# A windowed-attention block on one core: five equal score sets of 64-key pieces, E by V in 64x32 tiles over two banks, masks as a minimum on VectorE

## The chip, the cores and the metric

The kernel runs on one core of one Trainium2 chip. The metric is the device time in microseconds, a median over several runs. One execution was also recorded by the hardware profiler; all rows of the profile come from that one.

The engines are named as in the profile: PE (matrix products; PEld is its loading of the stationary operand, which is counted apart and overlaps), DVE (vector), ACT (activation functions and copies), POOL (general), SP (here it only issues DMAs). Matrix products write to PSUM, from which DVE and ACT read; all else lies in SBUF, 128 partitions wide. ACT and POOL can issue DMAs too; the profile then calls them ACTq and POOLq, as it calls SP's SPq.

## The reference

The block computes attention and an MLP, both behind a layer norm whose scale, shift and gate come from a vector c:

```python
mod = (_silu(c) @ w_mod).reshape(c.shape[0], 6, 1, -1)     # sa, ca, ga, sb, cb, gb
h = _layernorm(x) * (1 + ca) + sa
x = x + ga * _A_ref(h, wqkv, wo)                            # attention
h = _layernorm(x) * (1 + cb) + sb
x = x + gb * _B_ref(h, w_gate, w_up, w_down)                # (sigmoid(h @ w_gate) * (h @ w_up)) @ w_down

# in _A_ref: S = 2048, D = 640, H = 32, Dh = 20, W = 256
q, k, v = (h @ wqkv) split into 3 x H heads of Dh
scores = einsum('bhqd,bhkd->bhqk', q, k) * Dh ** (-0.5)
mask = (idx[:, None] - idx[None, :] >= 0) & (idx[:, None] - idx[None, :] < W)
p = softmax(where(mask, scores, -1e9))
o = einsum('bhqk,bhkd->bhqd', p, v) -> (S, D) @ wo
```

Each query sees itself and the 255 keys before it. x is 2048 x 640, the MLP's inner width is 1536, all inputs are bf16.

## The kernel before

The 2048 tokens are cut in eight chunks a = 0 to 7 of 256. A chunk goes through: layer norm statistics and normalisation (`ln_stats`, L785 ff., the normalised x is written at L815), turning to hT with tokens in columns and applying scale and shift (`modulate`, `pe_transposes`), projections to q, k and v with evictions from PSUM (`evac`, L914 on ACT, L915 on DVE), attention, the output projection, the second norm, the MLP (gate and up products in `h2T` by `wg` and `wu`, then `hh` by `wd`), and the gated sums. Weights are loaded once. The modulation vectors are computed at the start and while chunk 0 runs; gates are folded into the weights wo and wd (L1333, L1270).

Attention of a chunk is done in two halves q of sixteen heads. Head 16q + 4j + k lies with its 20 rows of Q and K at partitions 32j, so four heads go through four row groups of PE together. The scores are computed with keys on partitions and queries on columns, so that exp's output E is at once the moving operand of E by V. A half's scores go set by set into one PSUM tile S of four banks (pool `p_S` holds one such tile, 2048 columns), and each set is emptied by one exp on ACT over 128 x 2048 (L1067, L1041, in chunk 0 L1104). No maximum is subtracted; a column of ones beside V gives the sum of a row.

For chunks 1 to 7 `main_set` computes for four heads everything but the two ends of the window, in 24 matmuls with 64 keys each, two column groups at a time; `ends_set` computes for all sixteen heads of the half the first and the last 64 columns, in 32 matmuls with 128 keys. Four main sets and one ends set make a half. The masks are POOL's affine_select: each main set has two that write 128 x 256 pieces to a buffer G (L1072) and two on 128 x 512 in place (L1076), each ends set two on 128 x 1024 (L1045). Chunk 0 has no keys before it, and six sets in all (`score_set`, masks at L1112).

`burst` multiplies E by V for a half: 64 matmuls (32 in chunk 0) with 128 keys on the rows and 32 columns of V as weights, in four column groups, into two PSUM banks X. With `AFTER = 1` the burst of a half stands right before the second score set of the next half (`with_pv`), in chunk 0 (`NOW = 1`) by itself. `norm` transposes the result and divides (L1162 to L1166).

On every engine the order is fixed. The program is recorded as operations with the engines they may go to; `PLAN`, a list of numbers (operation times five plus engine), sets on which engine each runs and in which order; buffers of a pool are handed out in that same order, and semaphore waits are worked out from the dependencies. So attention's matmuls stand among those of the MLP and of the projections of neighbouring chunks, which fill PE while ACT works on a set. A list `FETCH` of 40 times stands for other DMA traffic in the planner's model of the DMA queues. POOL's operations also wait for the last DVE operation marked `port` before them. All of PE's products are issued by two helpers, `mm` at L698 (128 x 128 tiles) and L699 (smaller tiles). All DMAs are issued at L584 and, transposing, at L822.

These lines give the pieces of a main set and E by V in the old form:

```python
    PIECES = (((0, 0, 0, 256, 0), (-1, 64, 0, 256, 256)), ((-1, 0, 0, 192, 256), (0, 64, 64, 192, 64)),
              ((1, 0, 128, 64, 448), (-2, 64, 64, 64, 0)))
...
                for kb, q0, n, side, c0 in ((0, 0, 256, 0, 0), (-2, 0, 128, 1, 0), (1, 128, 128, 1, 128), (-1, 0, 256, 0, 256)):
...
                        ins = mm(e, X[bank].ap[32 * j:32 * j + 32, oc:oc + n], V[2 * a + kb].ap[:, h * VW:h * VW + 32],
                                 src, (bank, j) not in seen, True, tp=(0, 32 * j))
```

## Time and profile before

| | us |
|---|---|
| median of three runs | 324.63 |
| the runs | 323.03 to 324.86 |
| span of the profiled execution | 321.8 |
| PE busy | 315.6 |
| ACT busy | 213.9 |
| DVE busy | 198.8 |
| POOL busy | 189.5 |
| 16 DMA engines, mean rate | 102 GB/s |

The span goes from the first to the last instruction of the profiled execution; the page gives no other time of that execution. Busy times are sums over an engine's instructions. In rows of groups, the parts are: line, engine, operation, output and inputs by their names, shapes, count, then busy time, the mean length of one in ns, and the idle time of the engine just before them with what ended it. A row of the timeline has the start, the length, the line and the count of instructions put together; the length of the last matmul of such a row reaches into the next row, since matmuls overlap, so a stretch is best measured from start to start.

### The profile page before, as it was taken

What the parts mean: (1) busy time and instruction counts of PE and PEld (TensorE: products, weight loads), DVE (VectorE), ACT (ScalarE), POOL (GpSimd) and SP (SyncE); (2) the same over time, 40 slices, a digit from 0 to 9 for tenths busy, and PEclk for the clock granted to TensorE, in tenths of its full rate; (3) what the DMA queues carried; (4) which work ended last, traced back from release to release, by engine and by line L of the source; (5) the groups of instructions that cost most, each with busy time, mean ns of one, the idle gap of its engine ahead of it and who ended that gap; (6) DMA issues with size and microseconds to landing.
All of it is one profiled execution on the core that took longest, in us unless ns stands there. A gap on an engine that the chain in (4) does not pass through costs nothing.

```text
span 321.8 us, 11465 instructions
## 1 busy us (share of the span) xinstructions
PE 315.6 (98%) x5045; PEld 236.8 (74%) x5045; DVE 198.8 (62%) x424; ACT 213.9 (66%) x229; POOL 189.5 (59%) x349
## 2 busy tenths in 40 slices
PE   6999999999999999999999999999999999999996
PEld 2677767677877777766777677877877777877885
DVE  4689987877886746584555555465534474386323
ACT  2699997877787986768686867676976746411220
POOL 3338759878768493949484848577575826601000
PEclk9999999999999999999999999999999999999999
DMA  7999999999922534126526100220800004002101
GB/s 249 348 262 278 223 179 248 194 225 295 206 36 43 88 75 55 44 63 108 77 19 111 37 22 2 63 42 25 132 18 4 22 22 104 20 5 61 43 0 41
DMA packets 62123, 32.92 MB, mean 102 GB/s; under 512 B 45946, under 2 KB 60794, under 8 KB 62074
## 3 DMA queue, kind: packets, MB, share of 16 engines
q1 hardware_dynamic: 59904, 29.73, 43.5%
q10 hardware_dynamic: 2170, 2.46, 2.8%
q8 instruction: 39, 0.64, 0.9%
q14 instruction: 10, 0.08, 0.1%
HBM read 18.68 MB, written 2.62 MB: 66 GB/s over the span
## 4 chain that ended last, share of the span: by engine, by line
PE 96%; DMA 1%; DVE 1%; ACT 1%; issue 0%; ACTq 0%
PE M L698 79%; PE S L699 8%; PE M L699 7%; DMA x<-in_A_x_dram 1%; ACT hT L831 1%; DVE st L793 1%; PE S L698 1%; PE S L690 0%; ACT stg L914 0%; ACTq L584 0%; DVE x L815 0%; DVE st L795 0%; ACT hT L914 0%; DVE x L1308 0%; DVE mA L778 0%
## 5 line engine op out<-in xcount | busy, mean ns | idle before, releaser
L1067 ACT ACTIVATE E<-S 128x2048 bf16<-128x2048 f32 x56 | 105.0, 1875 | 40.6 <-PE S L699 40.2
L1072 POOL TENSOR_SCALAR_AFFINE_SELECT E<-E 128x256 bf16<-128x256 bf16 x112 | 46.6, 427 | 57.1 <-ACT E L1067 25.1
L1076 POOL TENSOR_SCALAR_AFFINE_SELECT E<-E 128x512 bf16<-128x512 bf16 x112 | 70.6, 646 | 4.6 <-DVE x L815 1.2
L698 PE MATMUL M<-h2T,wg 128*128 128x256 bf16 x480 | 67.0, 273 | 0.0
L698 PE MATMUL M<-h2T,wu 128*128 128x256 bf16 x480 | 66.7, 273 | 0.0
L1289 DVE SCALAR_TENSOR_TENSOR hh<-sig,M 128x512 bf16<-128x512 f32 x48 | 32.4, 678 | 42.9 <-ACT sig L1287 26.4
L698 PE MATMUL M<-wd,hh 128*128 128x320 bf16 (+2 forms) x396 | 57.1, 295 | 0.0
L698 PEld LDWEIGHTS M<-h2T,wg 128*128 128x128 bf16 x480 | 45.4, 98 | 7.8 <-DVE T L1162 0.2
L698 PEld LDWEIGHTS M<-h2T,wu 128*128 128x128 bf16 x480 | 45.2, 98 | 7.3
L1287 ACT ACTIVATE sig<-M 128x512 f32<-128x512 f32 x48 | 28.5, 595 | 31.2 <-PE M L698 30.9
L698 PEld LDWEIGHTS M<-wd,hh 128*128 128x128 bf16 x396 | 37.2, 98 | 13.7 <-DVE hh L1289 0.2
L1045 POOL TENSOR_SCALAR_AFFINE_SELECT E<-E 128x1024 bf16<-128x1024 bf16 x28 | 32.0, 1147 | 4.9 <-ACT E L1041 3.4
L699 PEld LDWEIGHTS S<-QT,KT 20*64 20x64 bf16 (+1 forms) x1856 | 20.0, 100 | 17.4 <-issue 9.7
L699 PE MATMUL S<-QT,KT 20*64 20x256 bf16 (+5 forms) x1856 | 32.3, 228 | 0.4 <-issue 0.4
L1041 ACT ACTIVATE E<-S 128x2048 bf16<-128x2048 f32 x14 | 26.3, 1876 | 6.8 <-PE S L699 6.7
L793 DVE BATCH_NORM_STATS2 st<-x 128x6 f32<-128x320 bf16 x64 | 28.9, 479 | 2.4 <-DMA x<-in_A_x_dram 1.8
L1162 DVE STREAM_TRANSPOSE T<-M 128x512 f32<-128x512 f32 x32 | 21.5, 700 | 12.9 <-PE S L699 11.6
L698 PE MATMUL M<-wk,hT 128*128 128x320 bf16 x160 | 27.9, 299 | 0.0
L1308 DVE TENSOR_TENSOR x<-M,x 128x320 bf16<-128x320 f32 (+2 forms) x33 | 15.4, 475 | 18.8 <-PE M L698 18.6
L698 PE MATMUL M<-wq,hT 128*128 128x320 bf16 x160 | 26.2, 299 | 0.7 <-DVE hT L832 0.5
L698 PE MATMUL M<-wv,hT 128*128 128x320 bf16 x160 | 26.0, 299 | 0.0
L698 PE MATMUL M<-wo,oT 128*128 128x320 bf16 x160 | 25.9, 299 | 0.0
(84 smaller groups left out, 356.4 us busy)
## 6 DMA issues: line engine op xcount, KB each, us to landing
x<-in_A_x_dram SPq DMA_DIRECT2D x18, 160.0 KB, 3.7
wd<-in_w_mod_dram SPq DMA_DIRECT2D x6, 320.0 KB, 5.4
wd<-in_B_w_down_dram SPq DMA_DIRECT2D x4, 480.0 KB, 5.5
wu<-in_w_mod_dram SPq DMA_DIRECT2D x5, 320.0 KB, 4.8
x<-in_A_x_dram ACTq DMA_DIRECT2D x8, 160.0 KB, 2.7
out_dram<-x SPq DMA_DIRECT2D x8, 160.0 KB, 1.9
wu<-in_B_w_up_dram SPq DMA_DIRECT2D x2, 576.0 KB, 4.7
wg<-in_B_w_gate_dram SPq DMA_DIRECT2D x2, 576.0 KB, 6.8
```

Of the source, the lines that this page charges most:

```text
L698: return e.matmul(o, l, r, start=st, stop=sp, skip_group_check=True)
L699: return e.matmul(o, l, r, start=st, stop=sp, tile_position=tp, skip_group_check=True)
L793: A("dve", lambda e, g, bi=bi, j=j: e.bn_stats(v(bi * 12 + j * 6, 6), src[bi].ap[:, j * 320:(j + 1) * 320]), 0.48, reads=[src[bi].r()], wr ...
L1041: A("act", lambda e, eng: e.activation(cell().rearrange("p m (x c) -> p m x c", c=64)[:, :, 0:4:3, :], Sp.ap[:].rearrange("p j (k x c) -> ...
L1045: A("pool", lambda e, eng, c0=c0, pat=pat, base=base, cm=cm: e.affine_select(cell()[:, :, c0:c0 + 64], cell()[:, :, c0:c0 + 64], pattern=p ...
L1067: A("act", lambda e, eng: e.activation(part(0, 512), Sp.ap[:], ACT.Exp, scale=SM_SCALE), 1.876, reads=[Sp.r()], writes=[E.r("C"), E.r("B") ...
L1072: A("pool", lambda e, eng, hc=hc, src=src, far_h=far_h: e.affine_select(side(hc), part(src, 64), pattern=[[0, 4], [-1 if far_h else 1, 64] ...
L1076: A("pool", lambda e, eng, c0=c0, near=near: e.affine_select(part(c0, 128), part(c0, 128), pattern=[[0, 4], [1 if near else -1, 128]], com ...
L1162: A("dve", lambda e, g, h=h: e.transpose(T1.ap[:, 512 * h:512 * h + 512], X[h].ap), 0.694, reads=[X[h].r()], writes=[T1.r(h)], prio=3.5, t ...
L1287: A("act", lambda e, g, pg=pg, sg=sg: e.activation(sg.ap[:], pg.ap[:], ACT.Tanh, scale=0.5), c_act(512), reads=[pg.r()], writes=[sg.r()], ...
L1289: A("dve", lambda e, g, pu=pu, sg=sg, f0=f0: e.scalar_tensor_tensor(out=hh.ap[:, f0:f0 + 2, :], in0=sg.ap[:].rearrange("p (a b) -> p a b", ...
L1308: A("dve", lambda e, g, ps=ps, bi=bi, c0=c0, n=n: e.tensor_tensor(x1[bi].ap[:, c0:c0 + n], ps.ap[:, 0:n], x1[bi].ap[:, c0:c0 + n], op=ALU. ...
```

## The change

For chunks 1 to 7 a half now has five equal score sets (`SETS`) in place of four and one. A piece is 64 keys by at most 256 queries, and each half of PE's columns (64 wide) takes its own heads. The first two sets have two pieces of 256 columns in each tile, the next two have pieces of 192, 64, 64 and 192, the fifth four of 128 (`ONE`, `TWO`, the last line of `SETS`). Chunk 0 has two sets of 192, 64 and 256 a half and one that both halves share. `run` issues the matmuls of the eight tiles in turn, by columns done. Over the whole program score matmuls go from 1856 to 1920.

E by V now uses tiles of 64 rows and 32 columns: each of the eight tiles (two row halves, four column groups) goes through the eight pieces of its head, the upper half of the rows into one PSUM bank of X and the lower into the other. A burst has 128 matmuls in place of 64 (64 in place of 32 in chunk 0), 1920 over the program in place of 960.

For this a head's V rows of one 64-key piece must lie in the right half of the partitions: the V projection reads wv's columns with a stride, and each V tile is evicted in twice as many pieces of 64 partitions (64 in place of 32).

The masks are a minimum of E with a table `mk`, on DVE: 79 tensor_tensor operations in place of POOL's selects. The table holds 0 or 3e38, and is made at the start by 9 instructions on POOL and DVE. G goes; there are 8 buffers for E in place of 6.

In `ln_stats` the normalisation of x may go to DVE or POOL for every chunk but the pieces done one by one at the start; with the new plan 12 of 32 are on DVE (26 before) and 20 on POOL (6 before).

```diff
-NE = 6
+NE = 8
 EW = 2048
+BIG = 3.0e38
...
+            if not one:
+                A("pool", lambda e, g: e.tensor_tensor(v(32, n), st.ap[:, 24:28].rearrange("p (b t) -> p b t", t=2)[:, :, 0], v(30, n),
+                                                       op=ALU.mult), 0.26,
...
+            A("dve" if one else ("dve", "pool"), xh, {"dve": 0.44, "pool": 0.87}, port=True,
...
-                    ps.ap[:, 0:320], hT[a].ap[:, kt, bi * 128:(bi + 1) * 128], wv[:, kt, half * 320:half * 320 + 320]))
+                    ps.ap[:, 0:320].rearrange("p (g c) -> p g c", c=40), hT[a].ap[:, kt, bi * 128:(bi + 1) * 128],
+                    wv[:, kt, :].rearrange("p (g c) -> p g c", c=80)[:, :, 40 * half:40 * half + 40])) for kt in range(NDT)]
...
+                for odd in range(2):
+                    evac(lambda b=b, half=half, odd=odd: heads(V[b].ap[64 * half:64 * half + 64, 352 * odd:352 * odd + 352], VW)[:, :, 0:DH],
+                         lambda ps=ps, odd=odd: heads(ps.ap[64 * odd:64 * odd + 64, 0:320], DH), 320, [ps.r()], [V[b].r((half, odd))], 6.5,
...
+    def run(e, prog, emit):
+        at = {t: p[0] for t, p in prog.items()}
+        pos = dict.fromkeys(prog, 1)
+        ins = None
+        while pos:
+            t = min(pos, key=lambda t: (at[t], list(prog).index(t)))
+            what = prog[t][pos[t]]
+            if isinstance(what, int):
+                at[t] = max(at[t], what)
+            else:
+                ins = emit(e, t, what)
+                at[t] += what[-1]
+            pos[t] += 1
+            if pos[t] == len(prog[t]):
+                del pos[t]
+        return ins
+
+    ONE = ((-1, 0), (0, 256))
+    TWO = ((-2, 0), (-4, 192), (3, 256), (1, 320))
+    SETS = (([(h, x, c) for x, c in st] for st in (ONE, TWO) for h in range(2)))
+    SETS = [list(x) for x in SETS] + [[(h, x, c + 256 * h) for h in range(2) for x, c in ((-3, 0), (2, 128))]]
+    MASKS = [(192, 512, 4, 128, 64)] * 2 + [(128, 512, 4, 256, 0)] * 2 + [(64, 256, 8, 128, 64)]
+    FIRST = ((1, 0), (3, 192), (0, 256))
+
+    def piece(x):
+        q0 = 64 * max(0, x)
+        return x // 2, x % 2, q0, 64 * min(4, x + 5) - q0
...
+            prog = {(j, half): [0] + [(q, h, x, c, piece(x)[3]) for q, h, x, c in parts] for j in range(4) for half in range(2)}
...
+                return mm(e, Sp.ap[64 * half:64 * half + 64, j, c:c + n], keys_of(a, kb, 64 * odd, gi, j, 64),
+                          QT[a].ap[32 * j:32 * j + DH, gi, q0:q0 + n], True, True, tp=(32 * j, 64 * half))
...
+                return e.tensor_tensor(v, v, mk[:, m0:m0 + w].unsqueeze(1).to_broadcast([128, g, w]), op=ALU.min)
+            A("dve", fn, c_dve(g * w, 2.0), port=True, reads=[E.r(), R_mk], writes=[E.r()], prio=5, tag=f"mask{a}")
...
+        mine = [(h, x) + where[a, q, h, x] for h in range(2) for x in ((-1, 0, -2, 1, -3, 2, -4, 3) if a else (0, 1, 2, 3))]
...
+                ins = mm(e, X[half].ap[32 * j:32 * j + 32, h * 256 + q0:h * 256 + q0 + n],
+                         V[2 * a + kb].ap[64 * half:64 * half + 64, v0:v0 + 32],
+                         E.ap[64 * half:64 * half + 64, j * 512 + c:j * 512 + c + n], t not in seen, True, tp=(64 * half, 32 * j))
```

`PLAN` is new as a whole. Its numbers count other operations than before, so its lines say nothing; the order that comes out of it does. In the changed kernel L706 and L707 are the two matmul helpers, L581 the DMAs, L1071 the masks, L920 the evictions on DVE, L1110 and L1112 `norm`'s first steps.

On PE, around a burst E by V of an early chunk, before (weights' and moving columns behind the names):

```order
L698 MATMUL M<-h2T,wg 128x256 x10
L699 MATMUL M<-E,V 32x256 x4
L699 MATMUL M<-E,V 32x128 x8
L699 MATMUL M<-E,V 32x256 x8
L699 MATMUL M<-E,V 32x128 x8
L699 MATMUL M<-E,V 32x256 x8
L699 MATMUL M<-E,V 32x128 x8
L699 MATMUL M<-E,V 32x256 x8
L699 MATMUL M<-E,V 32x128 x8
L699 MATMUL M<-E,V 32x256 x4
L699 MATMUL S<-QT,KT 64x256 x8
L699 MATMUL S<-QT,KT 64x192 x8
```

and of the changed kernel, with the score set that follows the burst:

```order
L707 MATMUL M<-E,V 32x256 x16
L707 MATMUL M<-E,V 32x192 x16
L707 MATMUL M<-E,V 32x128 x16
L707 MATMUL M<-E,V 32x64 x16
L707 MATMUL M<-E,V 32x256 x16
L707 MATMUL M<-E,V 32x192 x16
L707 MATMUL M<-E,V 32x128 x16
L707 MATMUL M<-E,V 32x64 x16
L707 MATMUL S<-QT,KT 64x256 x16
L706 MATMUL M<-wd,hh 128x320 x8
L706 MATMUL M<-wo,oT 128x320 x5
```

The burst stands at the same place, ahead of a score set, with twice the matmuls, in pieces of 256, 192, 128 and 64 columns; the set behind it has 16 matmuls there in place of 24.

The masks on POOL before, with a step of the norm (L800, L802) between them:

```order
L1072 AFFINE_SELECT E<-E 128x4x64 x2
L800 TENSOR_SCALAR st<-st 128x2
L1076 AFFINE_SELECT E<-E 128x4x128 x2
L802 TENSOR_TENSOR st<-st,mhalf 128x2
L1072 AFFINE_SELECT E<-E 128x4x64 x3
L1045 AFFINE_SELECT E<-E 128x16x64
```

and on DVE in the changed kernel, about chunk 0's end:

```order
L1071 TENSOR_TENSOR E<-E,mk 128x4x256 x2
L803 BN_AGGR st<-st 128x2
L1186 TENSOR_TENSOR x<-M,x 128x320
L1071 TENSOR_TENSOR E<-E,mk 128x4x128
L920 CAST V<-M 64x16x20
L1186 TENSOR_TENSOR x<-M,x 128x320
L1071 TENSOR_TENSOR E<-E,mk 128x8x128
```

The masks have moved from a queue with little beside them to the one that also evicts V and adds the residual (L1186).

On SP the first DMAs, before:

```order
L584 DMA wq<-in_A_wqkv_dram 128x3x320
L584 DMA x<-in_A_x_dram 128x640
L584 DMA wd<-in_w_mod_dram 128x1280 x5
L584 DMA wq<-in_A_wqkv_dram 128x5x320
L584 DMA wq<-in_A_wqkv_dram 128x2x320
```

and in the changed kernel (wd is here a buffer that w_mod goes through):

```order
L581 DMA wk<-in_A_wqkv_dram 128x5x320
L581 DMA x<-in_A_x_dram 128x640
L581 DMA wd<-in_w_mod_dram 128x1280 x5
L581 DMA wq<-in_A_wqkv_dram 128x3x320
L581 DMA x<-in_A_x_dram 128x640
```

A half of wk has come to the front, and the first part of wq stands behind w_mod.

248 lines of the change are left out of this document (77 added, 171 removed), and 217 rows, old and new, of the table PLAN.

## Prediction

> **What bounds the kernel now.** I read the page first: the busy line, the slices of PE and the shares of the chain.
>
> ```profile
> span 321.8 us, 11465 instructions
> PE 315.6 (98%) x5045; PEld 236.8 (74%) x5045; DVE 198.8 (62%) x424; ACT 213.9 (66%) x229; POOL 189.5 (59%) x349
> ...
> PE   6999999999999999999999999999999999999996
> ...
> PE 96%; DMA 1%; DVE 1%; ACT 1%; issue 0%; ACTq 0%
> ```
>
> Then the table of busy time by stretch (columns: PE, PEld, DVE, ACT, POOL with instruction counts, then the granted clock, the DMA share and GB/s).
>
> ```profile
> 0.00:14.00 14.00, 10.54 (x94) 5.42 (x95) 6.62 (x23) 5.61 (x12) 5.28 (x24) 1.00 0.91 292
> 14.00:50.00 36.00, 35.60 (x603) 25.26 (x603) 32.01 (x76) 33.34 (x43) 22.71 (x40) 1.00 1.06 243
> 50.00:100.00 50.00, 50.00 (x866) 36.89 (x864) 39.43 (x92) 39.07 (x41) 38.53 (x70) 1.00 0.91 188
> 300.00:321.80 21.80, 19.41 (x178) 16.55 (x176) 6.45 (x12) 3.59 (x6) 0.00 (x0) 1.00 0.08 24
> ```
>
> PE idles 3.5 us in the first 14, 2.4 in the tail, 0.4 between 14 and 50 and not at all from 50 to 300, at full clock. The time is therefore startup, plus the PE work, plus the tail. What PE no longer has to do is gained; work on another engine is free until PE waits for it. The span of 321.8 lies 2.8 below the median of 324.63, and I carry this 2.8 over.
>
> **E by V.** The PE timeline around one burst (start, length, instructions):
>
> ```profile
> 105.49 1.50 PE L699 MATMUL M<-E,V 128*32 128x256 bf16 x64
> 106.93 0.43 PE L699 MATMUL S<-QT,KT 20*64 20x256 bf16 x24
> 107.29 0.61 PE L698 MATMUL M<-h2T,wg 128*128 128x256 bf16 x4
> 107.73 1.04 PE L698 MATMUL M<-h2T,wu 128*128 128x256 bf16 x8
> 108.61 0.82 PE L698 MATMUL M<-h2T,wg 128*128 128x256 bf16 x6
> 109.39 0.41 PE L699 MATMUL S<-QT,KT 20*128 20x64 bf16 x32
> 109.74 0.39 PE L698 MATMUL M<-h2T,wu 128*128 128x256 bf16 x2
> ```
>
> Start to start, a burst takes 106.93 − 105.49 = 1.44 us. Eight matmuls of 256 columns take 108.61 − 107.73 = 0.88 us, or 0.43 ns a column. Each of the four old tiles streams 4 × (256+128+256+128) = 3072 columns, 1.32 us; the other 0.12 is the change of tiling. Each of the eight new tiles streams 4 × (256+192+128+64) = 2560 columns, since pieces of 64 keys skip more that is masked: 1.10 + 0.12 = 1.22 us, and 0.01 more for starting eight tiles. That is −0.21 a burst, and −2.9 for the fourteen of chunks 1 to 7. Chunk 0's two bursts go from 1536 to 1280 columns a tile, 0.11 less each: −0.2. Sum −3.1.
>
> **Scores.** A main set takes 107.29 − 106.93 = 0.36 us, an ends set 109.74 − 109.39 = 0.35, with about 0.1 of change each. For chunks 1 to 7 five sets stay five, at 0.36: +0.01 × 14 = +0.1. Chunk 0:
>
> ```profile
> 29.25 0.88 PE L699 MATMUL M<-wu,silubc 128*32 128x160 bf16 x40
> 29.95 0.83 PE L699 MATMUL M<-E,V 128*32 128x256 bf16 x32
> 30.71 0.62 PE L698 MATMUL M<-ident,stg 128*128 128x128 bf16 x8
> 31.30 0.40 PE L699 MATMUL S<-QT,KT 20*128 20x128 bf16 x16
> 31.63 0.40 PE L698 MATMUL M<-ident,stg 128*128 128x128 bf16 x4
> ```
>
> Six sets at 31.63 − 31.30 = 0.33 and a change become five at 0.36: about −0.3. Together −0.2. The rest of PE's matmuls is the same in number and columns; the V projection only reads its moving operand with a stride (runs of 40). Of the forty modulation matmuls in the first row above, half read theirs in runs of 32 (L735); in four tiles they take 29.95 − 29.25 = 0.70 us, 1600 columns a tile, 0.44 ns each, the same as contiguous ones. I cost it at nothing.
>
> **Masks and side work.** These are the groups of exp and three of the masks:
>
> ```profile
> L1067 ACT ACTIVATE E<-S 128x2048 bf16<-128x2048 f32 x56 | 105.0, 1875 | 40.6 <-PE S L699 40.2
> L1072 POOL TENSOR_SCALAR_AFFINE_SELECT E<-E 128x256 bf16<-128x256 bf16 x112 | 46.6, 427 | 57.1 <-ACT E L1067 25.1
> L1076 POOL TENSOR_SCALAR_AFFINE_SELECT E<-E 128x512 bf16<-128x512 bf16 x112 | 70.6, 646 | 4.6 <-DVE x L815 1.2
> L1045 POOL TENSOR_SCALAR_AFFINE_SELECT E<-E 128x1024 bf16<-128x1024 bf16 x28 | 32.0, 1147 | 4.9 <-ACT E L1041 3.4
> ...
> L1270 DVE TENSOR_TENSOR wd<-wd,gbc x11: 481/483/997, 68.9 to 92.7; 128x640 bf16<-128x640 bf16 x11
> ...
> L815 DVE TENSOR_SCALAR x<-x,st x26: 384/446/600, 7.0 to 294.0; 128x640 bf16<-128x640 bf16 x26
> ...
> L915 DVE CAST V<-M x23: 428/482/492, 20.2 to 182.8; 128x320 bf16<-128x320 f32 x23
> ```
>
> POOL loses 46.6 + 70.6 + 32.0 = 149 us and a little more in chunk 0. DVE gains 79 minima. L1270's 483 ns for 640 bf16 elements is 0.75 ns an element; so 512, 1024 and 256 take about 0.39, 0.77 and 0.19, and 32, 42 and 5 of them 46 us. Of V's 32 more evictions DVE takes 10 (+4.8) and ACT 22, fourteen normalisations of x leave DVE for POOL (14 × 0.45 = −6.2), and so do the five scalings of wo (−2.4, priced as L1270); casts that move between DVE and ACT cancel within 2. DVE comes to about 240 of 320 us, POOL to about 65; ACT loses one exp of 1.88 and some hT work, and stays near 214. None of it is on PE's path while the masks of a half are done before its burst; as that burst stands behind the second set of the next half, two exps of 1.88 us and PE's filler matmuls cover a mask of 0.4 to 0.8. The tight place is 14 to 50 us, where DVE was busy 32.0 of 36: cover there is thin. Upper bound +5 (below, rival D); below nothing is excluded, since PE had only 0.4 us to win there.
>
> **Startup.** SP now sends half of wk (400 KB) before x and the five w_mod loads, where it sent part of wq (240 KB).
>
> ```profile
> 11.71 2.06 PE L698 MATMUL M<-wq,hT 128*128 128x320 bf16 x14 [0.49 <-DVE hT L832]
> ...
> GB/s 249 348 262 278 223 179 248 194 225 295 206 36 43 88 75 55 44 63 108 77 19 111 37 22 2 63 42 25 132 18 4 22 22 104 20 5 61 43 0 41
> ...
> wk<-in_A_wqkv_dram SPq DMA_DIRECT2D x2, 400.0 KB, 6.3
> ...
> wq<-in_A_wqkv_dram SPq DMA_DIRECT2D x1, 240.0 KB, 2.7
> ```
>
> 160 KB at the 348 GB/s of the second slice is up to +0.5 for x and w_mod; a startup PE stall saved could make it −0.3. I take +0.2. The tail is unchanged.
>
> So far: −3.1 − 0.2 + 0.2 ≈ −3.1.
>
> **Where PE's instructions come from.** PE's one idle gap after the start (first row PEld with its wait in brackets), PE's instruction queue, and a small write:
>
> ```profile
> 42.85 0.11 PEld L699 LDWEIGHTS S<-QT,KT 20*64 20x64 bf16 x3 [0.56 <-issue]
> 42.85 0.22 PE L699 MATMUL S<-QT,KT 20*64 20x64 bf16 x3 [0.40 <-issue]
> ...
> q8 instruction: 39, 0.64, 0.9%
> ...
> out_dram<-x SPq DMA_DIRECT2D x1, 32.0 KB, 1.5
> ...
> 37.65:42.80 5.15, 4.81 (x141) 3.28 (x129) 4.69 (x12) 5.06 (x6) 3.32 (x7) 1.00 1.14 194
> 241.10:245.07 3.97, 3.97 (x130) 3.28 (x130) 2.30 (x6) 2.10 (x2) 0.71 (x2) 1.00 0.02 4
> ```
>
> The gap has no releaser ("issue") and comes in the middle of a score set. Queue 8 brought 39 packets of 16 KB for 2 × 5045 PE instructions, about 259 each, so I read them as blocks of 256. Counted in PE's order, the gap falls just behind instruction 1217 = 193 + 4 × 256, a block's end. I conclude that PE holds two blocks and that a block is fetched while the one before runs. The block that ran from 37.65 to the gap lasted 5.2 us with DMA full, and the next was 0.56 late; the block from 241.10 ran 3.97 us with DMA quiet and cost nothing. A block's fetch therefore takes between 1.5 (the 32 KB write) and 4.0 us with quiet DMA. Queue 8's 0.9% of 16 × 321.8 us is 1.2 us a packet; with about 1.3 for issue and landing as in that write, I take 2.5, an estimate.
>
> Now a burst is 128 matmuls and as many loads: one block in 1.23 us instead of half a block in 1.44. Counting the new program's order, the 16 bursts put block ends close behind the start of four: 49 instructions in at about 51 us, 33 at 118, 50 at 137, and 3 before one at 264. The block that then runs takes 2.2, 1.4, 2.1 and 1.5 us by the prices above. At 2.5 the waits are 1.1 at 118, 0.4 at 137 and 1.0 at 264; at 51 us, with DMA share 0.91, I take 3.7 for the fetch and 1.5 for the wait. Sum +4.0; the old gap of 0.56 goes. With 1.5 everywhere it is about +0.2, with 4.0 about +10. A block may also fall kindlier or worse than I count by a few waits.
>
> [...]
>
> **Forecast (B).** −3.1 − 0.6 + 4.0 = +0.3 on 321.8, 322.1 profiled, and 2.8 on top: about 325.0. B's own range is 322.2 (1.5 a fetch) to 330.
>
> **The rivals.**
>
> A: the clean gain. Fetches are always in time; −3.1 (and not −0.6 with it, since the gap may come elsewhere): 321.5. For it: one gap in 39 crossings before. Against it: no block ran under 3.97 us before. Chance 0.30.
>
> C, slower: PE cannot issue the burst that fast. Before, 128 instructions went in 1.44 us, 11 ns each; a score set of 64 in 0.35 us, 5.5 each. The new burst needs 1.23 / 256 = 4.8 ns each. If issue takes 7 ns, a burst lasts 256 × 7 = 1.8 us, +0.36 on the old, × 14 = +5.0 instead of −2.9: 324.63 + 5.0 + 0.1, 329.7. It decides from 1.44 / 256 = 5.6 ns. For it: 5.5 held for 64 instructions only, a quarter of a burst. Against it: loads and matmuls overlapped there without a gap. Chance 0.10.
>
> D: DVE is late. If the minimum, which repeats one table over four to sixteen groups, runs at half the speed of L1270, it is +46 us of DVE, 286 of 320, and from 14 to 50 us the masks hold up chunk 0's and 1's bursts: some six waits of 0.8, +5 on A's 321.5, 326.5. Against it: L1270 also reads two bf16 operands at speed. Chance 0.10.
>
> E: the weight load of 64 rows.
>
> ```profile
> L699 PE MATMUL M<-E,V 128*32 128x256 bf16 x480 | 22.3, 274 | 0.0
> ...
> L699 PE MATMUL S<-QT,KT 20*64 20x256 bf16 x448 | 17.7, 292 | 0.0
> ```
>
> The 64-wide score weights lengthen a matmul by 292 − 274 = 18 ns, so the round of 64 columns (64 × 0.43 = 28 ns) should hide a load; if loads of short rounds show with 24 ns, two rounds in 28 sets are +1.3: 322.9. Chance 0.05. [...]
>
> **How the numbers follow.** B has 0.45 and is the forecast. 1% (3.25 us) is about what a measurement of this kernel can tell from no change: faster is under 321.4, slower over 327.9. Faster: 0.6 of A, which stands at that bound (0.18), a tenth of B (0.05) and half of E (0.02), 0.25. Slower: 0.22 of B, for slow fetches (0.10), 0.9 of C (0.09) and 0.3 of D (0.03), 0.22. The rest, 0.53, is the same. The range runs from 320.8, A with a better start and no old gap, to 329.0, B with fetches of about 3.5; out are some of A's and B's ends and two thirds of C, 0.17.
>
> **What would show it.** E-V bursts of 1.23 us start to start with no gap inside would confirm the first term; 1.4 or more, evenly, is C. Gaps of 0.4 to 1.5 us on PE released by "issue", inside or just behind bursts near 51, 118, 137 and 264 us, are B; none is A. A PE wait for DVE's masks is D. The first projection matmul stood at 11.7 us and tells the startup. B is wrong if PE's idle time between 14 and 318 us stays under 1 us.

## The result, and the profile after

The changed kernel takes 347.25 us, the kernel before 324.19: a ratio of 1.068, 95% interval 1.061 to 1.075. The ratios here and below leave out executions that fell into a slower state (one of four here), the medians in us do not. It is slower by 7%, where the prediction had no change as the likeliest case and 329 us as the upper end of its range. The profiled execution of the changed kernel spans 346.5 us, 24.7 more than before.

The page of the changed kernel, the parts that answer to those of before (busy time, slices of PE and of its clock, the instruction queue of PE, the chain):

```profile
span 346.5 us, 13386 instructions
PE 323.7 (93%) x6068; PEld 236.7 (68%) x6069; DVE 236.6 (68%) x493; ACT 213.0 (61%) x231; POOL 110.2 (32%) x148
...
PE   6989866998998999979999999999999799999997
PEclk9999996999999999989999999999999989999999
...
q8 instruction: 47, 0.77, 1.0%
...
PE 67%; POOL 9%; DVE 8%; DMA 5%; ACT 4%; issue 3%; SPq 2%; ACTq 0%; POOLq 0%; DVEq 0%
```

PE is no longer busy throughout: PE's share of the chain falls from 96% to 67%, POOL and DVE have come into it, and the clock has three slices below full. The table by stretch, PE alone (busy, matmuls, granted clock, DMA):

```profile
14.00:50.00 36.00, 32.42 (x684) 1.00 0.75 201
50.00:100.00 50.00, 43.03 (x911) 0.93 0.84 181
100.00:150.00 50.00, 48.69 (x1069) 1.00 0.45 79
150.00:200.00 50.00, 46.93 (x899) 0.97 0.30 51
200.00:250.00 50.00, 49.94 (x1085) 1.00 0.33 59
250.00:300.00 50.00, 47.79 (x956) 0.97 0.14 36
```

Between 14 and 300 us PE idles 3.58 + 6.97 + 1.31 + 3.07 + 0.06 + 2.21 = 17.2 us, where it idled 0.4 before. The clock costs 50 x 0.07 + 50 x 0.03 + 50 x 0.03 = 6.5 us more, where it was full before; 1.1 of that falls on idle time. That is 22.2 of the 24.7. The rest is not idle time: PE idles 3.0 us before 14 and 2.6 us after 300, where it idled 3.5 and 2.4. So the question is what PE waits for. The longest wait by its releaser (total, times, longest):

```profile
PE M L706 <- POOL wo L1277: 5.9, 1, 5.9
```

and, in the chain of waits, the four longest pieces in which PE waited for nothing that the profile shows (start, length):

```profile
82.65 1.26 issue
...
149.91 2.04 issue
...
173.56 0.83 issue
...
275.23 2.21 issue
```

One wait of 5.9 us is for POOL, and these 6.3 us have no releaser; the other 5 us are waits of up to 1.1 us, most of them for DVE and POOL. The wait for POOL ends at 55.09 us, and the clock behind it is at half:

```profile
56.00:58.00 2.00, 2.00 (x10) 0.50 1.16 284
```

In the trace it stays so from 52.97 to 59.80 us; PE works from 55.09 on and loses 2.4 us by it. POOL's timeline up to the end of the wait:

```profile
42.26 1.40 POOL L1277 TENSOR_TENSOR wo<-wo,gbc 128x640 bf16<-128x640 bf16 x1 [5.25 <-DMA wo<-in_A_wo_dram]
43.63 5.00 POOL L820 TENSOR_SCALAR x<-x,st 128x640 bf16<-128x640 bf16 x2
48.59 6.35 POOL L1277 TENSOR_TENSOR wo<-wo,gbc 128x640 bf16<-128x640 bf16 x4
```

The row of x's normalisation on POOL in the changed kernel (count, then the least, median and longest in ns):

```profile
L820 POOL TENSOR_SCALAR x<-x,st x20: 2498/2509/2790, 16.3 to 314.4; 128x640 bf16<-128x640 bf16 x20
```

and in the kernel before:

```profile
L812 POOL TENSOR_SCALAR x<-x,st x6: 873/878/879, 25.7 to 74.3; 128x640 bf16<-128x640 bf16 x6
```

The same 128x640 normalisation took 878 ns there, and takes 2509 now. The rows differ in their last arithmetic step. Before, POOL multiplied and added a negated product; the change multiplies and subtracts the product.

A burst, and another with one of the waits without a releaser behind it, on PE's timeline:

```profile
95.70 1.48 PE L707 MATMUL M<-E,V 64*32 64x256 bf16 x128
97.11 0.42 PE L707 MATMUL S<-QT,KT 20*64 20x256 bf16 x16
...
148.07 1.48 PE L707 MATMUL M<-E,V 64*32 64x256 bf16 x128
149.49 0.42 PE L707 MATMUL S<-QT,KT 20*64 20x256 bf16 x16
151.95 0.59 PE L706 MATMUL M<-h2T,wg 128*128 128x256 bf16 x2 [2.04 <-issue]
```

and the four microseconds behind it in the table by stretch:

```profile
152.00:156.00 4.00, 4.00 (x47) 0.58 0.95 98
```

A burst takes 97.11 − 95.70 = 1.41 us, not 1.23. Behind a burst and a score set PE stands still for 2.04 us, and then the granted clock is near half: 0.42 × 4 = 1.7 us more are lost.

### The profile page after: what moved, and what is told of

Read it like the earlier page. It is cut to its first block, busy times and chain, and to the rows that moved or that the text cites. A ratio compares the mean times of both kernels' runs of the same rounds, so it can differ in the third digit from the quotient of the medians.

```text
span 346.5 us, 13386 instructions
## 1 busy us (share of the span) xinstructions
PE 323.7 (93%) x6068; PEld 236.7 (68%) x6069; DVE 236.6 (68%) x493; ACT 213.0 (61%) x231; POOL 110.2 (32%) x148
## 4 chain that ended last, share of the span: by engine, by line
PE 67%; POOL 9%; DVE 8%; DMA 5%; ACT 4%; issue 3%; SPq 2%; ACTq 0%; POOLq 0%; DVEq 0%
PE M L706 56%; PE S L707 6%; POOL x L820 5%; PE M L707 5%; ACT E L1066 2%; DMA hT<-x 2%; POOL wo L1277 2%; DMA wo<-in_A_wo_dram 2%; DVE st L801 2%; DVE E L1071 2%; SPq L581 1%; DMA x<-in_A_x_dram 1%; DVE stg L920 1%; DMA h2T<-x 1%; DVE V L920 1%
## 5 line engine op out<-in xcount | busy, mean ns | idle before, releaser
L1066 ACT ACTIVATE E<-S 128x2048 bf16<-128x2048 f32 x75 | 140.7, 1877 | 52.4 <-PE S L707 49.7
L706 PE MATMUL M<-h2T,wu 128*128 128x256 bf16 x480 | 69.5, 277 | 2.3 <-issue 2.1
L706 PE MATMUL M<-h2T,wg 128*128 128x256 bf16 x480 | 68.1, 273 | 2.0 <-issue 2.0
L706 PE MATMUL M<-wd,hh 128*128 128x320 bf16 (+2 forms) x396 | 61.5, 301 | 0.1
L706 PEld LDWEIGHTS M<-h2T,wu 128*128 128x128 bf16 x480 | 46.0, 99 | 12.7 <-issue 3.4
L706 PEld LDWEIGHTS M<-h2T,wg 128*128 128x128 bf16 x480 | 45.7, 98 | 10.3 <-issue 2.8
L820 POOL TENSOR_SCALAR x<-x,st 128x640 bf16<-128x640 bf16 x20 | 50.3, 2522 | 4.8 <-DVE x L820 2.1
L1071 DVE TENSOR_TENSOR E<-E,mk 128x1024 bf16<-128x1024 bf16 (+2 forms) x79 | 45.4, 591 | 8.4 <-ACT E L1066 8.0
L706 PEld LDWEIGHTS M<-wd,hh 128*128 128x128 bf16 x396 | 37.9, 99 | 14.6 <-issue 0.6
L706 PE MATMUL M<-wo,oT 128*128 128x320 bf16 x160 | 27.7, 305 | 5.9 <-POOL wo L1277 5.9
L707 PE MATMUL S<-QT,KT 20*64 20x64 bf16 (+3 forms) x1920 | 32.5, 237 | 0.3 <-ACT E L1066 0.2
L845 POOL TENSOR_SCALAR h2T<-h2T,scB,shB 128x256 bf16<-128x256 bf16 x18 | 10.0, 562 | 66.5 <-DVE E L1071 43.2
L1110 DVE STREAM_TRANSPOSE T<-M 128x512 f32<-128x512 f32 x32 | 21.5, 698 | 13.3 <-PE S L707 12.5
L808 POOL TENSOR_SCALAR st<-st 128x2 f32<-128x2 f32 (+1 forms) x17 | 3.9, 231 | 83.7 <-DVE st L803 67.8
L706 PE MATMUL M<-wv,hT 128*128 128x320 bf16 x160 | 29.4, 310 | 0.9 <-DVE T L1110 0.9
L706 PE MATMUL M<-wk,hT 128*128 128x320 bf16 x160 | 28.0, 300 | 1.8 <-DVE V L920 1.1
L707 PEld LDWEIGHTS S<-QT,KT 20*64 20x64 bf16 x1920 | 17.2, 104 | 16.2 <-issue 6.7
L706 PE MATMUL M<-wq,hT 128*128 128x320 bf16 x160 | 28.0, 299 | 0.0
```

What stands on the lines that cost most here:

```text
L706: return e.matmul(o, l, r, start=st, stop=sp, skip_group_check=True)
L707: return e.matmul(o, l, r, start=st, stop=sp, tile_position=tp, skip_group_check=True)
L820: return e.tensor_scalar(dst[bi].ap[:], src[bi].ap[:], v(30 + bi, 1), v(32 + bi, 1), op0=ALU.mult, op1=ALU.subtract)
L845: return e.tensor_scalar(ap, ap, sc[:, dt:dt + 1], sh[:, dt:dt + 1], op0=ALU.mult, op1=ALU.add)
L1066: A("act", lambda e, eng: e.activation(E.ap.rearrange("p (j c) -> p j c", j=4), Sp.ap[:], ACT.Exp, scale=SM_SCALE), 1.876, reads=[Sp.r()], ...
L1071: return e.tensor_tensor(v, v, mk[:, m0:m0 + w].unsqueeze(1).to_broadcast([128, g, w]), op=ALU.min)
```

## The experiments

Theory P says that the subtracting form on POOL is slow and holds up PE; theory I that the many instructions of the new bursts are the cost, by late blocks of instructions and the half clock behind them; theory D, the rival, that DVE with the masks is late.

**The adding form put back.**

```diff
-                A("pool", lambda e, g: e.tensor_tensor(v(32, n), st.ap[:, 24:28].rearrange("p (b t) -> p b t", t=2)[:, :, 0], v(30, n),
-                                                       op=ALU.mult), 0.26,
+                def neg(e, g):
+                    for bi in range(n):
+                        ins = e.tensor_scalar(v(32 + bi, 1), v(24 + 2 * bi, 1), v(30 + bi, 1), -1.0, op0=ALU.mult, op1=ALU.mult)
+                    return ins
+                A("pool", neg, 0.26,
...
-                return e.tensor_scalar(dst[bi].ap[:], src[bi].ap[:], v(30 + bi, 1), v(32 + bi, 1), op0=ALU.mult, op1=ALU.subtract)
+                return e.tensor_scalar(dst[bi].ap[:], src[bi].ap[:], v(30 + bi, 1), v(32 + bi, 1), op0=ALU.mult, op1=ALU.add)
```

> The changed kernel with one form put back: the normalisation of x on POOL multiplies and adds a negated product, as the kernel before did, where the change multiplies and subtracts. Theory P (the 2.51 us of that POOL row is the form): the row falls to about 0.88 us, so 20 x 1.63 = 33 us leave POOL; PE's 6.2 us behind the scaling of wo shrinks by the two normalisations queued ahead of it, 3.3 us, or goes, the half clock behind it goes (about 3 us), and the waits for x at 65, 105, 123 and 314 us go; 347.3 becomes 328 to 334, with the four waits of PE for instructions (6.3 us) still there. Theory D (DVE's masks hold POOL back, the form costs nothing): the row stays over 2 us and the time over 342. Theory I (instruction supply alone): the row falls, but the time stays over 342.

340.5 us, ratio to before 1.052 (1.049 to 1.055). The row of the normalisation:

```profile
L823 POOL TENSOR_SCALAR x<-x,st x20: 868/873/1445, 18.0 to 306.2; 128x640 bf16<-128x640 bf16 x20
```

and PE's waits:

```profile
PE M L706 <- issue: 5.5, 4, 2.0
...
PE M L707 <- issue: 2.1, 1, 2.1
...
PE M L706 <- POOL wo L1280: 0.6, 1, 0.6
```

The row falls to 873 ns and the wait for wo to 0.6: the form is what made POOL slow. But by the ratios only about 5 us came back (1.068 to 1.052), not the 13 to 19 expected, and the waits without a releaser have grown to 7.6.

**The subtracting form in the kernel before**, in its six normalisations on POOL.

```diff
-                A("pool", lambda e, g, bi=bi: e.tensor_scalar(st.ap[:, 32 + bi:33 + bi], v(24 + 2 * bi, 1), v(30 + bi, 1), -1.0,
+                A("pool", lambda e, g, bi=bi: e.tensor_scalar(st.ap[:, 32 + bi:33 + bi], v(24 + 2 * bi, 1), v(30 + bi, 1), 1.0,
...
-                    return e.tensor_scalar(dst[bi].ap[:], src[bi].ap[:], v(30 + bi, 1), v(32 + bi, 1), op0=ALU.mult, op1=ALU.add)
+                    return e.tensor_scalar(dst[bi].ap[:], src[bi].ap[:], v(30 + bi, 1), v(32 + bi, 1), op0=ALU.mult, op1=ALU.subtract)
```

> The kernel before with its six POOL normalisations of x in the changed kernel's form: the product is not negated, and the last step subtracts it. Nothing else moves, and DVE has no masks. Theory P: the six rows rise from 0.88 to about 2.5 us, 10 us more of POOL; the time is the same or up to 3 us longer, since POOL's masks are then late at three places. Theory D (the length comes from masks on DVE): the rows stay at 0.88 us.

331.8 us against 323.57, ratio 1.024 (1.020 to 1.027). The row:

```profile
L812 POOL TENSOR_SCALAR x<-x,st x6: 2492/2515/2520, 25.4 to 82.8; 128x640 bf16<-128x640 bf16 x6
```

and the two longest waits of PE:

```profile
PE M L699 <- POOL E L1076: 2.8, 1, 2.8
PE M L698 <- DVE stg L915: 2.6, 1, 2.6
```

Without one mask on DVE the row goes from 878 to 2515 ns: the length belongs to the form. That six such rows cost 8.2 us, and not at most 3, was missed: they make PE wait twice for over 2.5 us, and 6.8 us at half clock (64.45 to 71.28 us; PE goes on at 65.03 and loses 3.1) come with the first wait, none with the second.

**Narrow pieces first**, in the kernel with the adding form.

```diff
-        mine = [(h, x) + where[a, q, h, x] for h in range(2) for x in ((-1, 0, -2, 1, -3, 2, -4, 3) if a else (0, 1, 2, 3))]
+        mine = [(h, x) + where[a, q, h, x] for w in (((-4, 3, -3, 2), (-2, 1, -1, 0)) if a else ((3, 2, 1, 0),)) for h in range(2) for x in w]
```

> As the kernel with the adding form, and the eight pieces of a burst in another order: the narrow ones of both heads first (64, 64, 128, 128 columns), the wide ones after. Theory Q (PE starts a burst out of a filled queue and then issues one matmul in 8.4 ns, so a round of eight takes 67 ns however narrow it is): the four narrow rounds and the next ones come out of the queue, the wide rounds of 80 and 107 ns hide the issue, and a burst takes 1.2 to 1.28 us start to start in place of 1.41, 2 to 3 us in all beside the kernel with the adding form. Theory S (the time of a burst is its columns plus a fixed change of tiling): 1.41 us as before and the same time within 1 us.

343.04 us, ratio 1.059 (1.054 to 1.064); the burst takes 1.42 us as before:

```profile
107.43 1.49 PE L707 MATMUL M<-E,V 64*32 64x64 bf16 x128
108.85 0.42 PE L707 MATMUL S<-QT,KT 20*64 20x256 bf16 x14
```

Theory Q's gain fails. In its trace the first 32 matmuls of the burst start in rounds of eight, 3 to 4 ns apart within a round; then PE stands for about 78 ns, and from there on matmuls start 8 to 9 ns apart, so that rounds of eight with 64 or 128 columns take 66 to 67 ns each. In the changed kernel's burst at 95.70 us the first 50 start at 3 to 4 ns within a round before the 8 to 9 begin. What ends the quick starts is not shown by any run. The waits without a releaser came to 10.3 us in this profile, 2.7 more than without the new order, which would account for the 2.5 us more in time; why there are more stays open.

**Met waits between the bursts**, to move the ends of the instruction blocks.

```diff
+                    pads = spread(ops) if e == "pe" else {}
                     for o in ops:
+                        for _ in range(2 * pads[o] + (not waits[o]) if pads.get(o) else 0):
+                            engine.wait_ge(h("act"), 1)
...
+PADGAP = [12, 0, 84, 134, 46, 16, 6, 82, 0, 0, 98, 26, 12, 12, 64, 52]
```

(Two such waits make one instruction in the trace; `spread` shares the numbers over PE's operations between the bursts.)

> The kernel with the adding form, and 644 waits on PE that are always met already, spread over the ordinary matmuls between the bursts (0 to 134 before each), so that from 95 us on a block of 256 PE instructions ends in the midst of a burst and no block runs under 3.8 us. Theory I (PE waits for instructions where a block runs under about 3.7 us, and the clock halves for 3.4 us behind such a wait of 2 us): the waits at 142, 166 and 268 us (2.1, 0.7 and 2.2) go and so do the two stretches of half clock (1.7 each), 8.4 in all, 340.5 to 332 or a little more for the waits' own cost; before 95 us, where DMA is busy, waits of 1 to 2 may stay. Rival R (the waits come from something else at these places, a semaphore or a buffer): they stay where they were and the time is 340 or more.

The profiled execution took 343.59 us, but the others scattered up to 352.85, so that no ratio can be given: it is not the gain that was expected. PE by stretch in that profile:

```profile
150.00:200.00 50.00, 49.24 (x1036) 1.00 0.29 50
200.00:250.00 50.00, 44.33 (x888) 0.97 0.36 53
```

From 150 to 200 us (and likewise from 100 to 150) the waits at bursts and the half clock are gone but for one wait of 0.4 us, as theory I has it. But two of 2.8 and 2.4 us, which end at 217 and 239, are new; there the trace shows the fetch of the next block begin 4.6 and 3.5 us behind the block's start instead of about 1. Why it began late stays open. And the met waits are not free: PE's busy time is 324.8 against 321.4, although less of it is at half clock. As a test of the total it is spoilt by its own cost.

**Wide and narrow by turns**, and **masks on 4 columns**, both with the met waits.

```diff
-            prog = {(half, j): [0] + [x + (piece(x[1])[3],) for x in mine] for half in range(2) for j in range(4)}
+            prog = {(half, j): [0] + [x + (piece(x[1])[3],) for x in (mine if half == 0 else mine[::-1])] for half in range(2) for j in range(4)}
```

```diff
-                v = E.ap.rearrange("p (g c) -> p g c", c=step)[:, :, c0:c0 + w]
-                return e.tensor_tensor(v, v, mk[:, m0:m0 + w].unsqueeze(1).to_broadcast([128, g, w]), op=ALU.min)
+                v = E.ap.rearrange("p (g c) -> p g c", c=step)[:, :, c0:c0 + 4]
+                return e.tensor_tensor(v, v, mk[:, m0:m0 + 4].unsqueeze(1).to_broadcast([128, g, 4]), op=ALU.min)
```

> As the kernel with the met waits, and the order of the pieces of a burst turned round in the lower half of the tiles, so that wide and narrow pieces are issued by turns. Theory Q (issue of 8.4 ns a matmul is hidden only beside wide pieces; with turns the eight tiles share it evenly): a burst goes from 1.41 to 1.2 to 1.3 us, 1.5 to 3 us in all beside the kernel with the met waits. Rival S (a burst costs 1.41 whatever the order, as the order with the narrow pieces first did): the same time within 1 us.

> As the kernel with the met waits, and each of the 79 minima on DVE works on 4 columns of each group in place of 64 to 256, which leaves most of the masking out of what is computed; its order and its waits stay. Theory D (DVE, full from 14 to 50 us, makes PE late): DVE loses about 35 us, the 1.6 us wait of PE for the eviction of KT at 43 goes and what the masks hold up behind it, 3 us or more in all. Theory N (the masks cost nothing that PE sees): within 1.5 us of the kernel with the met waits.

The first took 349.76 us, ratio 1.078 (1.071 to 1.085). A burst takes 1.36 us (most of those in the trace that have no wait inside), so turns gain 0.05, not 0.1 to 0.2. The second took 347.0, 1.067 (1.061 to 1.073). Since the kernel that both stand beside scatters by 9 us, neither total says anything about order or masks; the masks were tried again below.

**The same columns in fewer instructions.** Five matmuls of 512 columns a tile in place of sixteen.

```diff
-            prog = {(half, j): [0] + [x + (piece(x[1])[3],) for x in mine] for half in range(2) for j in range(4)}
+            Es = list(dict.fromkeys(x[2] for x in mine))
+            cols = [512] * 5 if a else [512, 512, 256]
+            prog = {(half, j): [0] + [(Es[i % len(Es)], n) for i, n in enumerate(cols)] for half in range(2) for j in range(4)}
...
+                ins = mm(e, X[half].ap[32 * j:32 * j + 32, 0:n], V[2 * a].ap[64 * half:64 * half + 64, v0:v0 + 32],
+                         E.ap[64 * half:64 * half + 64, j * 512:j * 512 + n], t not in seen, True, tp=(64 * half, 32 * j))
```

> The kernel with the adding form, and in each burst the same 2560 columns a tile in five matmuls of 512 in place of sixteen narrow ones (chunk 0: 512, 512, 256): 40 matmuls, 80 instructions, in place of 128 and 256. What is multiplied is no longer attention; tiles, banks, columns, order and waits stay. Theory I (the many instructions of the burst are the cost: issue in the burst, late blocks behind it, half clock behind a late block): a burst takes 1.2 to 1.25 us (-0.2 x 14 = -2.7), PE waits for instructions less than 0.5 us in all from 95 us on and has no half clock there (-4.9 and -3.4), and little before; 340.5 becomes 326 to 330. Rival R (other things make PE late and the instruction waits are a sign of it): the bursts get shorter but the waits move, 336 or more.

325.23 us, ratio to before 1.006 (1.004 to 1.008): 15.3 us less than with the adding form alone. A burst:

```profile
85.53 1.27 PE L707 MATMUL M<-E,V 64*32 64x512 bf16 x40
86.74 0.42 PE L707 MATMUL S<-QT,KT 20*64 20x256 bf16 x16
```

PE by stretch, where the changed kernel had lost most:

```profile
50.00:100.00 50.00, 49.50 (x827) 1.00 0.92 175
```

and its instruction queue:

```profile
q8 instruction: 37, 0.61, 0.8%
```

With the columns unchanged a burst takes 1.21 us, PE is busy and at full clock from 14 us on, and all waits of over 0.2 us without a releaser are gone. Theory I holds. What is left over the kernel before is 1.7 us.

**Gaps of three lengths in the kernel before.**

```diff
-                    for o in ops:
+                    for i, o in enumerate(ops):
+                        for _ in range(2 * HOLD.get(i, 0) + 1 if e == "pe" and i in HOLD else 0):
+                            engine.wait_ge(h("act"), 1)
...
+HOLD = {380: 60, 520: 120, 680: 240}
```

> The kernel before, with 60, 120 and 240 waits that are always met put at three places of PE's order (at about 135, 182 and 233 us), in one clump each, so that PE has gaps of three lengths where it had none. Theory C (a gap of PE of some 2 us or more is followed by 3.4 us at half clock): behind the gaps longer than 2 us the granted clock reads 0.5 for about 3.4 us, behind shorter ones 1.0. Rival K (the half clock belongs to the 64x32 bursts): the clock stays at 1.0 everywhere, since the kernel before has none.

373.04 us, in a single execution. The first clump on PE's timeline:

```profile
131.66 1.11 PE L703 MATMUL M<-wq,hT 128*128 128x320 bf16 x7
137.78 0.96 PE L703 MATMUL M<-wq,hT 128*128 128x320 bf16 x3 [5.00 <-issue]
```

and PE and its clock by stretch:

```profile
136.00:140.00 4.00, 2.22 (x9) 0.62 0.00 0
140.00:144.00 4.00, 4.00 (x40) 0.53 0.00 0
144.00:148.00 4.00, 4.00 (x105) 1.00 0.17 43
```

The clock halves in the kernel that had none of it, at each of the three gaps (0.50 from 136.97, 191.58 and 259.85 us on); rival K falls. An instruction that carries two met waits turned out to cost about 0.1 us (24.8 us for 240), so no gap was shorter than 5 us, and this run does not tell what a shorter one does. At the first gap the clock was full again at 143.79 us, 6 us after work resumed.

**All block ends moved by 121 instructions**, in the kernel with the adding form.

```diff
+                    held = [o for o in ops if o.tag == "fill"][-1:]
                     for o in ops:
+                        for _ in range(2 * SHIFT + (not waits[o]) if e == "pe" and o in held else 0):
+                            engine.wait_ge(h("act"), 1)
...
+SHIFT = 121
```

> The kernel with the adding form, and 121 met waits in one clump before the first projection, so that every block of 256 PE instructions ends 121 instructions earlier in the program than it did; nothing else moves. Theory I: the waits for instructions at 142, 166 and 268 us go, and one comes that was not there, of about 2 us at the burst near 190 us (the third boundary from 173 us on), with smaller ones before 95 us at other bursts than 60 and 78. Rival R: waits stay at 142, 166 and 268. The time says little, between 333 and 343.

350.94 us, ratio 1.084 (1.079 to 1.089): more than the 333 to 343 expected. The clump itself takes 12.5 us ahead of the first projection and is followed by half clock up to 27.5 us, so all places lie some 11 us later than expected. At the burst for which a wait of 2 us was foretold:

```profile
208.76 1.48 PE L713 MATMUL M<-E,V 64*32 64x256 bf16 x128
210.17 0.30 PE L713 MATMUL S<-QT,KT 20*64 20x256 bf16 x5
212.43 0.41 PE L713 MATMUL S<-QT,KT 20*64 20x256 bf16 x11 [1.96 <-issue]
```

It came there, and none came at the three bursts where the unmoved kernel had them. A longer one, of 3.2 us, came at another burst, at 85 us, where small ones were expected. The waits follow the ends of the blocks. Counted through the traces, the weight loads, matmuls and waits of PE taken together, the waits without a releaser of 0.4 us or more end at instruction 193 + 256 n, give or take one record that a trace lacks: at 1217 in the kernel before (42.85 us), at 2753, 5569, 6337 and 10689 in the changed one (83.9, 152.0, 174.4 and 277.4 us), and by the same count the 1.96 us here and the 2.02 us at 60 us with the adding form. Only clumps of met waits stand elsewhere.

**Masks again**, in the kernel with wide matmuls: the same edit as above.

> The kernel with five wide matmuls a tile in each burst, and each of the 79 minima on 4 columns of each group in place of 64 to 256 (most of the masking is left out of what is computed). With PE's waits for instructions gone, what the masks cost on DVE can be read. Theory D: DVE loses about 30 us and PE's small waits for exp and evictions between 28 and 50 us (0.5, 0.3, 0.6) go, 1 to 3 us below 325.2. Theory N: within 1 us of 325.2.

325.26 us, ratio 1.006 (1.003 to 1.009), beside 325.23. DVE has 203.8 us of work in place of 233.8, and the time is the same within about 1 us: 30 of the 45 us of masks on DVE cost nothing here. Theory D falls.

**The subtracting form again**, in the kernel with wide matmuls (the adding form undone).

> The kernel with five wide matmuls a tile in each burst, and the normalisation on POOL in the changed kernel's subtracting form. Beside 325.2 this prices the form alone. Theory P: the row is 2.5 us again and PE waits behind the scaling of wo by two normalisations, 3.3 us more than the 0.6 before, and 1 to 2 us at two or three other places, with half clock behind the longest: 332 to 337. Rival: the form costs little once instructions come in time, under 328.

333.92 us, ratio 1.032 (1.027 to 1.037): by the ratios the form alone costs 8.5 us here. It does so in more places than expected: PE waits 1.8 us behind the scaling of wo, where theory P had 3.9, and three times for 1.2 to 1.6 us elsewhere; half clock follows one of these.

**Twice the instructions in the kernel before**, with the same products.

```diff
-                    for j in range(4):
+                    for c in (0, n // 2):
+                        for j in range(4):
...
-                        ins = mm(e, X[bank].ap[32 * j:32 * j + 32, oc:oc + n], V[2 * a + kb].ap[:, h * VW:h * VW + 32],
-                                 src, (bank, j) not in seen, True, tp=(0, 32 * j))
+                            ins = mm(e, X[bank].ap[32 * j:32 * j + 32, oc + c:oc + c + n // 2], V[2 * a + kb].ap[:, h * VW:h * VW + 32],
+                                     src[:, c:c + n // 2], (bank, j) not in seen, True, tp=(0, 32 * j))
```

> The kernel before, with each matmul of a burst of chunks 1 to 7 cut in two halves of its columns: 128 matmuls and 256 instructions a burst in place of 64 and 128, with the same products, columns, tiles, order and waits. Theory I: 128 x 8.4 = 1.08 us of issue stays under the burst's 1.44, which therefore hardly grows, but blocks now run in 1.5 to 3 us at some bursts: PE waits for instructions 2 to 3 us near 57 us, about 2 at 157 and 173, and 1 at three other places, 7 to 11 in all, with half clock behind some: 323.6 becomes 331 to 338. Rival R (the number of instructions doesn't matter): within 1.5 us of 323.6.

340.03 us as the median; the ratio is 1.038 (1.033 to 1.043), some 336 us. A burst without a wait, and one with:

```profile
112.15 1.54 PE L699 MATMUL M<-E,V 128*32 128x128 bf16 x128
113.62 0.43 PE L699 MATMUL S<-QT,KT 20*64 20x256 bf16 x24
...
162.48 1.49 PE L699 MATMUL M<-E,V 128*32 128x128 bf16 x124
166.31 0.24 PE L699 MATMUL M<-E,V 128*32 128x128 bf16 x4 [2.34 <-issue]
```

and PE's waits:

```profile
PE S L699 <- issue: 3.9, 3, 2.2
PE M L698 <- issue: 2.5, 2, 2.3
PE M L699 <- issue: 2.3, 1, 2.3
```

The burst itself hardly grows (1.47 us), and 8.7 us of waits without a releaser appear that the kernel before does not have, by nothing but the count of instructions. The granted clock of this execution is 0.99: behind two of them it is at half for 3.4 us each, which costs 3.4 us; 8.7 + 3.4 makes the 12 us that the total lies above the 323.62 of before.

None of these kernels that computes the block beats the kernel before.

**The sum.** By the ratios to the kernel before the changed kernel lies 22 us above it. Of these the adding form gives about 5 (1.068 to 1.052, uncertain by 2.5), and fewer instructions for the same columns 15 more (1.052 to 1.006): 7.6 of waits, 3.4 of half clock and 14 × 0.2 of shorter bursts in that kernel's profile make 13.8 of them. In the other order it is about 12 for the instructions (1.068 to 1.032) and 8.5 for the form; the difference between the orders, some 3 us, is little more than these ratios can tell. The masks cost nothing that the runs can tell. What is left over the kernel before's 323.55 is 1.7.

## Why the prediction was wrong

**The POOL operation that arrived was not priced.** The step "fourteen normalisations of x leave DVE for POOL (14 × 0.45 = −6.2)" counts what DVE loses and gives POOL "about 65" without showing a term for what arrives. At the adding form's 878 ns, which a row of the kernel before shows, the fourteen are 14 × 0.88 = 12 us. But the diff also shows the last step of the operation change from an add to a subtract, which I took for the same; the 0.87 that the diff gives as its time on POOL is the adding form's. It is 2.51 us, 50.3 us for the twenty and POOL 110.2 in all; with the adding form POOL has 82.3, so "about 65" left out other arrivals too. "None of it is on PE's path" was argued for the masks alone; x's normalisation stands on POOL ahead of the scaling of wo, and PE waited 5.9 us there, with 4.7 us at half clock behind it (2.4 lost).

**The first term, −3.1, was almost nothing.** The column count was right: 2560 columns in 40 instructions take 1.21 us, as forecast. As 256 instructions they take 1.41, so the burst gained 0.03 and not 0.21. This is rival C's mechanism with a smaller size: 1.41 / 256 is 5.5 ns an instruction, just at the 5.6 from which C was said to decide. It was wrong to hold C and the forecast apart: the issue rate did not make the burst longer than before, but took its gain.

**Forecast B had the mechanism, and was too small in three ways.** Counted in instructions it was right: of the four bursts named with a block's end close by, the second, third and fourth have the wait, at 149.9, 173.6 and 275 us. (The microseconds that I gave for them, 118, 137 and 264, were too early.) At the first, whose block ends at 62.6 us, PE waited 0.5 for hT on POOL instead; with the adding form the wait without a releaser is there, 2.02 us at 58 to 60. One at 82 us was not named. But they are 2.04, 0.83 and 2.21 where I had 1.1, 0.4 and 1.0, 6.3 in all for 4.0, and the half clock comes on top. First, a fetch took longer than the 2.5 us that I estimated from the write and the packet's 1.2 us: at the last three of the four waits the packet of queue 8 started 0.9 to 1.3 us behind the block's first instruction, took 0.9 to 1.4, and PE went on 1.2 to 1.5 us after its end, 3.5 to 3.9 in all. My upper bound of 4.0 held these three; I chose the wrong end. It is no fixed time: the block from 130.56 us ran 2.42 us without a wait behind it, and there the packet started at 130.49, ahead of the block's first instruction. Second, the half clock behind the waits of 2.04 and 2.21 us, 1.7 us a time, was in no term: the row of the kernel before reads 1.00 throughout, and nothing bounded what a gap would do to it. Third, one more wait came than I named: from 78.73 to 83.91 us, with a DMA share of 1.09, the packet started 2.5 us behind the block's first instruction, and from block to block it took 5.2 us; it took 4.9 at 77 us in the kernel with the adding form. The bounds of B's own range do not follow from its terms either: −3.1 − 0.6 + 0.2 on 324.6 is 321.1, and with +10 it is 330.9, where the text has 322.2 and 330.

**Rival A fell.** It had every fetch in time, 321.5 us. The changed kernel lost 6.3 us at crossings from block to block, and the kernel before, with the instructions of its bursts doubled, has 8.7 us of waits without a releaser; the one that ends at 166.3 us stands at instruction 6081 = 193 + 23 × 256.

**What was right.** The masks (45.4 us of DVE for 46 forecast, and no cost in time), DVE's total (236.6 for 240), the scores, the V projection with its stride (299 ns a matmul with the adding form, as before), and start and tail (5.6 us of idle time for 5.9). Rival E did not show: its 24 ns for a load in a short round were supposed, and no run shows them; a score set with two rounds of 64 columns takes 0.36 us (82.00 to 82.36), as a main set did.

## What to carry to other kernels

When work moves to another engine, price every instruction that arrives there by a row of that very form, down to its last arithmetic step: an add turned into a subtract made a POOL operation three times as long (878 to 2509 ns). When a dense piece is cut into more instructions, count instructions as well as columns: against the pace of issue inside the piece, and against the time from block to block, at three waits of the changed kernel 3.5 to 3.9 us for 256, and 5.2 at a fourth, where the fetch began 2.5 us behind the block's first instruction. In the changed kernel a gap of 2.04 us cost 3.7, since 3.4 us at half clock followed it.

## What the runs showed of the hardware that was not expected

On POOL a tensor_scalar of 128x640 bf16 with multiply and subtract took 2509 to 2515 ns, with multiply and add 873 to 878 (medians of two kernels each way).

In the changed kernel's burst at 95.70 us PE started the first 50 matmuls 3 to 4 ns apart within a round of eight, and later ones 8 to 9 ns apart; with the narrow pieces first it was 32. The second round of eight tiles with 64 columns there took 66 ns, where 64 columns at 0.43 ns are 28.

A gap of PE of about 2 us halved its clock for 3.4 us in some places and not in others: after waits of 2.04 and 2.21 us in the changed kernel it did, after one of 2.02 at 60 us in the kernel with the adding form and 1.96 in the one with moved blocks it did not. The clock records of seven traces (the changed kernel; the adding form; the subtracting form in the kernel before; narrow pieces first; wide matmuls; the three gaps; the moved blocks) show where such gaps lay. Half clock comes in them in stretches of 3.41 us (one, two, four or eight of them on end, the last of the changed kernel cut short by the trace's end), and those of one trace begin whole multiples of 3.41 us apart. If each trace is divided into such stretches, then where PE at full clock idled more than 2.0 us within one, the next was at half clock each time; under 1.5 us never; in between both occur (with narrow pieces first 1.88 us at 57 us was followed by half clock, 1.91 at 142 us was not). A stretch at half clock was followed by another also with less idle time in it: 0.6 us in the kernel before with the subtracting form, 0.8 and 1.3 in the one with three gaps. The 2.04 and 2.21 us lie within one stretch each. The 2.02 us fall in two, 0.57 and 1.46, and so do the 1.96, 1.31 and 0.65, and the second wait of 2.76 us in the kernel before with the subtracting form, 1.87 and 0.89.

An instruction of PE that carries nothing but two semaphore waits that are already met cost 0.10 us in a clump (12.5 us for 121, 24.8 for 240).
